# Attention and a GELU feed-forward layer on one core: scores of batch 2, two GpSimd copies and the w_out loads move

## The chip, the cores and the metric

The kernel runs on one core of one Trainium2 chip. The metric is the device time of one execution, in microseconds. The kernel before was timed five times. One execution of it was recorded by the hardware profiler, and all durations below come from that record.

## The reference

For each of 8 batches and 8 heads, a sequence x (512 x 64) and a state (32 x 64) attend to each other. Both results are concatenated along the sequence, the heads are joined into 512 columns, and a two-layer network with exact GELU follows. Cut to what matters:

```python
scores = scale * x @ state.T          # 512 x 32 per batch and head
a      = softmax(scores)
xread  = a @ state                    # 512 rows
scores2 = scale * state @ x.T
sread  = softmax(scores2) @ x         # 32 rows
y = concat([xread, sread], rows), heads joined   # 4352 x 512
h = y @ w_in                          # 512 -> 2048
out = gelu(h) @ w_out                 # 2048 -> 512, float32
```

## The kernel before

**The work of one batch.** The scores of a batch are exponentiated once into e (`scores`, L315: 16 small matmuls into two PSUM tiles pt, and two exps on ScalarE). `norm` (L337) divides by the row sums on VectorE, in two halves, and gives a. The reads of the sequence rows are not formed: state and w_in are multiplied first into P (`pmat`, L428, four pieces of 512 columns, copied out of PSUM by ScalarE and VectorE), and the hidden layer is then AT times P, where AT is a transposed. For batches from 2 on, AT is made by a DMA transpose on SP's queue (`atr_dma`, L363), and the transposed x that the scores need by another (`xtr_dma`, L268).

`mm1(b, m)` (L464) makes one of 16 row blocks of the hidden layer: two matmuls into a PSUM tile hp, and a gelu on ScalarE into row m of gs[b]. `M(k)` is mm1 with k = 16 b + m, so M(22) is row 6 of batch 1. The second layer is done in units: `U(u)` is mm2(u // 16, u % 16 // 4, u % 4), and mm2(b, q, j) (L490) multiplies the four rows m = 4 q to 4 q + 3 of gs[b] with the same rows of w_out, for one block j of 128 tokens, into one PSUM tile. U(20) is therefore mm2(1, 1, 0): rows 4 to 7 of batch 1. `mm2_m(b, m)` (L518) does one row m for all four blocks j instead. The units serve batches 0 and 1; from batch 2 on the second layer is formed with seven half-size products (`X`, L602), whose sums of w_out (`w_sums`, L545) are made once on VectorE.

`sread` (L371) multiplies e with a copy of x that has a column of ones beside it (xo). That copy is made by `rearr_ones` (L223), on GpSimd from batch 2 on, and the copy x4 that the DMA transpose reads by `rearr` (L214), on GpSimd too. Both kinds of buffer have two copies, taken in turn by the batch number.

**What sets the order.** The schedule is written out by hand (`tc.manual_schedule()`): each engine executes its instructions in the order of the calls, and semaphores are set where one engine reads what another wrote. The calls from L805 to L939 are the first two batches, the loop from L942 does the rest. PSUM tiles with the tag "f" (hp, pt, p_ps and others) come from four slots taken in turn: a new one waits until the fourth before it has been read.

**Loads.** All weights and the x of batches 1 to 7 are loaded by DMAs that GpSimd issues, in the order of the calls. `load_rest` (L133) issues the second to fourth chunks of w_in and w_out, the rest of the state, and x of batches 2 and 3. On GpSimd's queue follow rearr(2), rearr_ones(2), a one-element copy called hold (L912, which waits for row 4 of gs[1]), load_x(4), rearr(3), rearr_ones(3), the hold of L975 (which waits for row 0 of gs[2]), load_x(5) and rearr(4).

Of the kernel before, what the change touches and what calls it, by code (L numbers as in the profile page):

```python
# [17 lines left out]
def kernel(  # L18
# [8 lines left out]
    nc = tc.nc  # L27
# [27 lines left out]
    def otile(shape, name, at=None):  # L55
        if at is None:
            at = turn[0] % 4
            turn[0] += 1
        return ps_o.tile(shape, FP32, name=name, tag=f"o{at}")
# [19 lines left out]
    hold = persist.tile([128, 1], BF16, name="hold")  # L79
# [23 lines left out]
    def load_w_in(f0, f1):  # L103
        for t in range(2):
            nc.gpsimd.dma_start(
                out=w_in_bf[64 * t:64 * t + 64, :, f0:f1],
                in_=moe_w_in[256 * t:256 * t + 256, f0:f1].rearrange("(c d) f -> d c f", c=HC),
            )
# [3 lines left out]
    def load_w_out(m0, m1):  # L112
        nc.gpsimd.dma_start(out=w_out_bf[:, m0:m1, :], in_=w_out_r[:, m0:m1, :])

    def load_x(b):
        xb = xin.tile([128, H, SJ * D], BF16, name="xb", tag="xb")
        nc.gpsimd.dma_start(out=xb, in_=xr[b])
        xbs[b] = xb

    def load_st(b0, b1):  # L120
        nc.gpsimd.dma_start(
            out=st_bf[:, b0:b1, :, :].rearrange("q b t d -> q (b t) d"),
            in_=st_rows[:, b0:b1, :, :].rearrange("q b t d -> q (b t) d"),
        )
# [6 lines left out]


    def load_rest():  # L133
        load_w_out(4, 8)
        for f in range(2, FC):
            load_w_in(512 * f, 512 * f + 512)
            load_w_out(4 * f, 4 * f + 4)
        load_st(2, B)
        load_x(2)
        load_x(3)  # L140
# [82 lines left out]
    def rearr_ones(b):  # L223
        A = atts[b]
        eng = nc.vector if b < 2 else nc.gpsimd
        src = xbs[b].rearrange("p (t c) (j d) -> p t c j d", t=2, d=D)
        for t in range(2):
            eng.tensor_copy(  # L228
                out=A.xo[:, :, :, 2 + 64 * t:66 + 64 * t].rearrange("p j c d -> p c j d"),
                in_=src[:, t],  # L230
            )
# [36 lines left out]
    def xtr_dma(b):  # L268
        A = atts[b]
        nc.sync.dma_start_transpose(  # L270
            out=A.xT.rearrange("p j c n -> p (j c) n"),
            in_=A.x4.rearrange("p j c n -> p (j c n)"),
        )
# [41 lines left out]
    def scores(b, half):  # L315
        A = atts[b]
        if half == 0:
            begin_e(b)
        pt = ps_f.tile([128, SJ, 2, 2, NS], FP32, name="pt", tag="f")
        for ci in range(2):  # L320
            c = 2 * half + ci
            for j in range(SJ):
                nc.tensor.matmul(  # L323
                    pt[:, j, :, ci, :],
                    lhsT=A.xT[:, j, c, :],
                    rhs=sbd[:, b, c, :],
                    start=True,
                    stop=True,
                )
        nc.scalar.activation(  # L330
            out=A.e[:, :, 64 * half:64 * half + 64],
            in_=pt.rearrange("p j t c n -> p (j t) (c n)"),
            func=AF.Exp,
            scale=scale,
        )

    def norm(b, half):  # L337
        A = atts[b]
        G = SJ * 2
        hs = slice(64 * half, 64 * half + 64)  # L340
        e4 = A.e[:, :, hs].rearrange("p g (c n) -> p g c n", n=NS)
        cs = att.tile([128, G, 2], FP32, name="cs", tag="cs")
        nc.vector.reduce_sum(out=cs, in_=e4, axis=AX.X)  # L343
        ics = att.tile([128, G, 2], FP32, name="ics", tag="ics")
        nc.vector.reciprocal(out=ics, in_=cs)
        nc.vector.tensor_tensor(  # L346
            out=A.a[:, :, hs].rearrange("p g (c n) -> p g c n", n=NS),
            in0=e4,
            in1=ics[:, :, :].to_broadcast((128, G, 2, NS)),
            op=ALU.mult,  # L350
        )
# [11 lines left out]
    def atr_dma(b):  # L363
        A = atts[b]
        A.AT = att.tile([128, SJ, 2, 128], BF16, name="AT", tag="AT")
        nc.sync.dma_start_transpose(
            out=A.AT.rearrange("p j t n -> p (j t) n"), in_=A.a
        )
# [29 lines left out]
    def srt(b):  # L398
        A = atts[b]
        ps = ps_f.tile([128, HC, NS], BF16, name="srT", tag="f")  # L400
        nc.tensor.transpose(
            ps.rearrange("p c n -> p (c n)"), A.srm.rearrange("q t d -> q (t d)"), ident
        )
        nc.vector.tensor_copy(out=XSR[:, :, :, b], in_=ps)
# [23 lines left out]
    def pmat(b, f):  # L428
        p_copy(b, f, p_mm(b, f, ftile))
# [32 lines left out]
    gs = {}  # L462

    def mm1(b, m):  # L464
        if m == 0:
            gs[b] = gpool.tile([128, MC, S], BF16, name="g", tag="g")
        hp = ps_f.tile([128, S], FP32, name="hp", tag="f")
        for t in range(2):
            nc.tensor.matmul(  # L469
                hp,  # L470
                lhsT=Ps[b][:, t, m * 128:(m + 1) * 128],
                rhs=atts[b].AT[:, :, t, :],
                start=(t == 0),
                stop=(t == 1),
            )
        nc.scalar.activation(out=gs[b][:, m, :], in_=hp, func=AF.Gelu)  # L476
# [13 lines left out]
    def mm2(b, q, j):  # L490
        if q == 0:
            ops[b, j] = otile([128, d_model], "op")
        ps = ops[b, j]
        for m in range(4 * q, 4 * q + 4):
            nc.tensor.matmul(  # L495
                ps,
                lhsT=gs[b][:, m, j * 128:(j + 1) * 128],
                rhs=w_out_bf[:, m, :],
                start=(m == 0),
                stop=(m == MC - 1),  # L500
            )
        if q == 3:
            rows = out_rows(b, j)
            evac(ps, [(rows, slice(0, 128), 0, d_model)])
# [13 lines left out]
    def mm2_m(b, m):  # L518
        for j in range(SJ):
            if m == 0:  # L520
                ops[b, j] = otile([128, d_model], "op")
            nc.tensor.matmul(  # L522
                ops[b, j],
                lhsT=gs[b][:, m, j * 128:(j + 1) * 128],
                rhs=w_out_bf[:, m, :],
                start=(m == 0),
                stop=(m == MC - 1),
            )
# [16 lines left out]
    def w_sums(i):  # L545
        (b11, b12), (b21, b22) = w_q
        w_add(*(
            ("3", b12, b22, ALU.subtract),
            ("4", b21, b11, ALU.subtract),
            ("6", b11, b12, ALU.add),  # L550
            ("1", b11, b22, ALU.add),
            ("7", b21, b22, ALU.add),
        )[i])
# [243 lines left out]
    def M(*ms):  # L797
        for m in ms:
            mm1(m // MC, m % MC)

    def U(*us):
        for u in us:
            mm2(u // 16, u % 16 // 4, u % 4)
# [24 lines left out]
    norm0(1)  # L828
    load_x(1)
    load_rest()  # L830
    nc.scalar.activation(out=gate, in_=gate, func=AF.Gelu)
    keep_warm(8)
# [38 lines left out]
    scores(1, 0)  # L871
    scores(1, 1)
    srt(0)
    U(4, 5)
    rearr_ones(1)
    U(6)
    pmat(0, 2)
    norm(1, 0)
    norm(1, 1)
    U(7)  # L880
    M(8, 9)
    sread(1)
    sread_out(1)
# [32 lines left out]
    begin(3)  # L916
    rearr(3)
    xtr_dma(3)
    rearr_ones(3)
    M(22, 23)  # L920
    scores(2, 0)
    scores(2, 1)
    U(18)
    norm(2, 0)
    norm(2, 1)
    M(24, 25)
    U(19)
    M(26, 27)
    U(20, 21)
    w_sums(1)  # L930
    M(28, 29)
    w_sums(2)
    U(22)
    atr_dma(2)
    M(30, 31)
    U(23)
    pmat(2, 3)
    w_sums(3)
# [118 lines left out]
```

## Time and profile before

| What | Value |
|---|---|
| median of five executions | 206.92 us |
| lowest and highest of the five | 206.73 and 207.49 us |
| profiled execution, whole | 207.19 us |
| its span, first to last instruction | 205.4 us |
| granted TensorE clock | 0.998 |
| TensorE, ScalarE, VectorE, GpSimd busy | 199.7, 133.0, 133.4, 61.7 us |
| one gelu of 128 x 512 on ScalarE (L476) | 601 ns, 124 of them |
| one activation table load on ScalarE | 1283 ns |
| one xo copy of GpSimd (L228), median | 1.04 us |
| AT by DMA, issue to landing, median | 3.7 us |

A line of a timeline gives the start, the length, the engine, the line of the kernel, the operation, what is written and read with shapes, how many instructions are merged, and in brackets the idle time before with the one who ended it. PE is TensorE, PEld its weight loads, ACT ScalarE, DVE VectorE, POOL GpSimd, SP the engine that issues the output and transposing DMAs. Matmuls overlap, so four of 0.38 us do not take 1.5 us: the distance from start to start counts.

### The profile page before, as it was taken

To read this page: it belongs to the slowest core of one execution; us is meant where nothing else is said; L and a number is where in the kernel's file an instruction comes from. 1 tells how busy PE (TensorE), PEld (TensorE's weight loads), DVE (VectorE), ACT (ScalarE), POOL (GpSimd) and SP (SyncE) were. 2 spreads that over 40 slices of the span, in tenths; PEclk is the share of its full clock that TensorE was granted. 3 is DMA by queue.
4 is the path that set the end of the run, shared out by engine and by line. 5 is a ranking of instruction groups with operands and counts; after the bars stand their busy time and mean duration, and the time that the engine had idled before them with its cause. 6 is when DMAs were issued, how large, how long until landed. Compare 5 with 4: busy or idle time off the path is not lost.

```text
span 205.4 us, 4667 instructions
## 1 busy us (share of the span) xinstructions
PE 199.7 (97%) x1952; PEld 132.2 (64%) x1959; DVE 133.4 (65%) x218; ACT 133.0 (65%) x241; POOL 61.7 (30%) x68
## 2 busy tenths in 40 slices
PE   7899999999999999999999999999999999999994
PEld 6554544444344567766775777667775788778893
DVE  2752575885776767976697757765778553165883
ACT  4574676679795879665967687587857476744120
POOL 8694300746060305271626602330220001200000
PEclk9999999999999999999999999999999999999999
DMA  5999999679655917742594405350109001030125
GB/s 191 204 195 180 199 195 193 113 232 164 97 63 144 228 28 99 161 152 56 67 151 142 106 0 116 112 134 3 51 10 199 3 0 51 3 153 0 54 99 158
DMA packets 39733, 23.14 MB, mean 113 GB/s; under 512 B 21792, under 2 KB 37792, under 8 KB 39712
## 3 DMA queue, kind: packets, MB, share of 16 engines
q0 software_dynamic: 13408, 8.10, 28.5%
q1 hardware_dynamic: 25616, 14.16, 28.5%
q10 hardware_dynamic: 688, 0.59, 0.8%
q8 instruction: 15, 0.25, 0.5%
q14 instruction: 6, 0.05, 0.1%
HBM read 17.30 MB, written 8.91 MB: 128 GB/s over the span
## 4 chain that ended last, share of the span: by engine, by line
PE 93%; DMA 4%; DVE 1%; SPq 0%; issue 0%
PE xp L577 34%; PE hp L469 26%; PE op L495 9%; PE p_ps L414 5%; PE op L522 3%; PE hps L509 3%; PE rp L753 3%; DMA x0f<-in_x_dram 3%; DMA AT<-a 2%; PE xp L683 2%; PE pt L323 2%; PE sr L377 1%; PE hp L848 1%; PE warm_ps L146 1%; PE aT_ps L360 1%; PE xT_ps L263 0%
## 5 line engine op out<-in xcount | busy, mean ns | idle before, releaser
L476 ACT ACTIVATE g<-hp 128x512 bf16<-128x512 f32 x124 | 66.9, 601 | 27.8 <-PE hp L469 22.2
L469 PE MATMUL hp<-AT,P 128*128 128x512 bf16 x248 | 63.6, 379 | 0.4 <-DMA AT<-a 0.3
L577 PEld LDWEIGHTS <-gsum 128*128 128x128 bf16 x448 | 43.4, 98 | 11.1 <-issue 1.9
L571 DVE TENSOR_TENSOR gsum<-g 128x2048 bf16<-128x2048 bf16 x30 | 38.6, 1305 | 0.1
L469 PEld LDWEIGHTS <-P 128*128 128x128 bf16 x248 | 22.8, 98 | 21.2 <-issue 2.5
L577 PE MATMUL xp<-ws,gsum 128*128 128x256 bf16 x256 | 30.6, 273 | 0.0
L426 DVE CAST P<-p_ps 128x512 bf16<-128x512 f32 x31 | 20.1, 685 | 10.5 <-PE p_ps L414 10.4
L495 PE MATMUL op<-w_out_bf,g 128*128 128x512 bf16 x91 | 22.9, 379 | 0.2
L577 PE MATMUL xp<-ws,g 128*128 128x256 bf16 x192 | 22.9, 273 | 0.0
L577 PE MATMUL xp<-w_out_bf,gsum 128*128 128x256 bf16 x192 | 22.8, 273 | 0.0
L425 ACT CAST P<-p_ps 128x512 bf16<-128x512 f32 x31 | 16.9, 596 | 7.6 <-PE p_ps L414 7.4
L577 PEld LDWEIGHTS <-g 128*128 128x128 bf16 x192 | 18.8, 98 | 4.3
L626 POOL TENSOR_TENSOR u<-s,oh 128x512 f32<-128x512 f32 x5 | 6.6, 1311 | 41.0 <-ACT oh L623 41.0
L228 POOL COPY xo<-xb 128x1024 bf16<-128x1024 bf16 x12 | 14.5, 1236 | 12.8 <-PE sr L377 12.8
L495 PEld LDWEIGHTS <-g 128*128 128x128 bf16 x96 | 9.0, 98 | 11.2 <-issue 1.1
L218 POOL COPY x<-xb 128x1024 bf16<-128x1024 bf16 x12 | 12.1, 1043 | 10.6 <-DMA xb<-in_x_dram 10.6
L596 POOL TENSOR_TENSOR v<-q,oh 128x512 f32<-128x512 f32 x5 | 7.1, 1428 | 20.8 <-ACT oh L628 20.8
L343 DVE TENSOR_REDUCE cs<-e 128x16 f32<-128x512 bf16 x14 | 9.5, 677 | 3.8 <-ACT e L330 3.8
L414 PE MATMUL p_ps<-w_in_bf,sbd 64*32 64x512 bf16 x256 | 10.9, 389 | 0.0
L620 DVE TENSOR_TENSOR s<-xp,s 128x512 f32<-128x512 f32 x5 | 3.5, 692 | 11.3 <-PE xp L577 11.3
L346 DVE TENSOR_TENSOR a<-e,ics 128x512 bf16<-128x512 bf16 x14 | 10.2, 730 | 0.5
L599 DVE TENSOR_TENSOR oh<-xp,v 128x512 f32<-128x512 f32 x5 | 3.5, 692 | 9.2 <-POOL v L596 9.2
(108 smaller groups left out, 220.2 us busy)
## 6 DMA issues: line engine op xcount, KB each, us to landing
xb<-in_x_dram POOLq DMA_DIRECT2D x7, 512.0 KB, 6.0
out_dram<-oh SPq DMA_DIRECT2D x13, 256.0 KB, 2.4
out_dram<-osb SPq DMA_DIRECT2D x10, 256.0 KB, 3.4
out_dram<-oh SPq DMA_DIRECT2D x5, 512.0 KB, 2.8
w_in_bf<-in_moe_w_in_dram POOLq DMA_DIRECT2D x8, 256.0 KB, 9.2
w_out_bf<-in_moe_w_out_dram POOLq DMA_DIRECT2D x3, 512.0 KB, 13.2
x0f<-in_x_dram ACTq DMA_DIRECT2D x2, 256.0 KB, 3.9
x0f<-in_x_dram SPq DMA_DIRECT2D x2, 256.0 KB, 4.6
```

Source lines behind the costliest of these rows:

```text
L218: nc.gpsimd.tensor_copy(out=A.x4[:, :, :, 64 * t:64 * t + 64].rearrange("p j c d -> p c j d"), in_=src[:, t],)
L228: eng.tensor_copy(out=A.xo[:, :, :, 2 + 64 * t:66 + 64 * t].rearrange("p j c d -> p c j d"), in_=src[:, t],)
L343: nc.vector.reduce_sum(out=cs, in_=e4, axis=AX.X)
L346: nc.vector.tensor_tensor(out=A.a[:, :, hs].rearrange("p g (c n) -> p g c n", n=NS), in0=e4, in1=ics[:, :, :].to_broadcast((128, G, 2, NS) ...
L414: nc.tensor.matmul(ps[t][32 * c:32 * c + 32, :], lhsT=sbd[64 * t:64 * t + 64, b, c, 32 * t:32 * t + 32], rhs=w_in_bf[64 * t:64 * t + 64, c ...
L425: nc.scalar.copy(out=dst[:, 0, :], in_=ps[0])
L426: nc.vector.tensor_copy(out=dst[:, 1, :], in_=ps[1])
L469: nc.tensor.matmul(hp, lhsT=Ps[b][:, t, m * 128:(m + 1) * 128], rhs=atts[b].AT[:, :, t, :], start=(t == 0), stop=(t == 1),)
L476: nc.scalar.activation(out=gs[b][:, m, :], in_=hp, func=AF.Gelu)
L495: nc.tensor.matmul(ps, lhsT=gs[b][:, m, j * 128:(j + 1) * 128], rhs=w_out_bf[:, m, :], start=(m == 0), stop=(m == MC - 1),)
L571: nc.vector.tensor_tensor(out=t, in0=g_q(b, h0, k0), in1=g_q(b, h1, k1), op=op)
L577: nc.tensor.matmul(ps[:, j - js[0], :], lhsT=lhs[:, m, 128 * j:128 * j + 128], rhs=rhs[:, m, :], start=(first and j == js[0] and m == 0), ...
```

## The change

Four things are edited. The w_out chunks of `load_rest` are loaded as two halves each. The second chunk of w_out is used row by row for batch 0: mm2_m(0, 4) to mm2_m(0, 7) stand where U(4) to U(7) stood. The two scores of batch 2 stand ahead of M(22,23) and not behind; the units U(19), U(20) and U(21) each stand one place further up between the pairs of M that follow. And rearr_ones(3) moves from behind xtr_dma(3) to behind M(30,31), with a new hold ahead of it that waits for row 15 of gs[1].

```diff
     def load_rest():
-        load_w_out(4, 8)
+        load_w_out(4, 6)
+        load_w_out(6, 8)
         for f in range(2, FC):
             load_w_in(512 * f, 512 * f + 512)
-            load_w_out(4 * f, 4 * f + 4)
+            load_w_out(4 * f, 4 * f + 2)
+            load_w_out(4 * f + 2, 4 * f + 4)
...
     srt(0)
-    U(4, 5)
+    mm2_m(0, 4)
+    mm2_m(0, 5)
     rearr_ones(1)
-    U(6)
+    mm2_m(0, 6)
     pmat(0, 2)
     norm(1, 0)
     norm(1, 1)
-    U(7)
+    mm2_m(0, 7)
...
     xtr_dma(3)
-    rearr_ones(3)
-    M(22, 23)
     scores(2, 0)
     scores(2, 1)
     U(18)
     norm(2, 0)
     norm(2, 1)
+    M(22, 23)
+    U(19)
     M(24, 25)
-    U(19)
+    U(20)
     M(26, 27)
-    U(20, 21)
+    U(21)
     w_sums(1)
     M(28, 29)
     w_sums(2)
     U(22)
     atr_dma(2)
     M(30, 31)
+    nc.gpsimd.tensor_copy(out=hold, in_=gs[1][:, 15, 0:1])
+    rearr_ones(3)
     U(23)
```

## The prediction

> **What bounds the kernel now.** I read the page's busy times first, then the waits of TensorE, then the timelines of the stretch that the change rewrites.
>
> ```profile
> PE 199.7 (97%) x1952; PEld 132.2 (64%) x1959; DVE 133.4 (65%) x218; ACT 133.0 (65%) x241; POOL 61.7 (30%) x68
> ```
>
> TensorE is busy 199.7 of 205.4 us. The same 1,952 matmuls stay, so a change of order can only remove or add time in which TensorE waits. The waits of TensorE (engine, line, releaser: total, times, longest) are these:
>
> ```profile
> PE warm_ps L146 <- DVE warm L92: 1.0, 1, 1.0
> PE xT_ps L250 <- DVE x0b L236: 0.4, 1, 0.4
> PE pc L284 <- DVE xT L253: 0.3, 1, 0.3
> PE hp L469 <- DMA AT<-a: 0.3, 1, 0.3
> ```
>
> Three lie in the first 9 us, which no edit touches. The fourth is the only one within reach: M(32) waits for the DMA that transposes batch 2's attention weights (atr_dma(2)). TensorE's timeline there (start, length, line, tiles, count):
>
> ```profile
> 44.62 0.41 PE L414 MATMUL p_ps<-w_in_bf,sbd 64*32 64x512 bf16 x8
> 44.97 1.04 PE L469 MATMUL hp<-AT,P 128*128 128x512 bf16 x4
> 45.84 0.63 PE L323 MATMUL pt<-sbd,xT 128*128 128x64 bf16 x16
> 46.30 1.03 PE L495 MATMUL op<-w_out_bf,g 128*128 128x512 bf16 x4
> 47.17 1.03 PE L469 MATMUL hp<-AT,P 128*128 128x512 bf16 x4
> 48.03 0.81 PE L495 MATMUL op<-w_out_bf,g 128*128 128x512 bf16 x3
> 48.90 1.03 PE L469 MATMUL hp<-AT,P 128*128 128x512 bf16 x4
> 49.76 1.89 PE L495 MATMUL op<-w_out_bf,g 128*128 128x512 bf16 x8
> ...
> 55.03 0.41 PE L414 MATMUL p_ps<-w_in_bf,sbd 64*32 64x512 bf16 x8
> 55.74 1.04 PE L469 MATMUL hp<-AT,P 128*128 128x512 bf16 x4 [0.30 <-DMA AT<-a]
> ```
>
> Read the starts, not the lengths: four matmuls take 0.863 us from start to start (48.90 to 49.76), 0.216 each; sixteen score matmuls take 0.46. After p_ps the next matmul starts 0.35 later (44.62 to 44.97), so M(32) was due at 55.03 + 0.35 = 55.38 and started at 55.74: the wait is worth 0.36. ScalarE in the same stretch:
>
> ```profile
> 45.10 0.59 ACT L425 CAST P<-p_ps 128x512 bf16<-128x512 f32 x1 [0.58 <-PE p_ps L414]
> 45.61 1.08 ACT L476 ACTIVATE g<-hp 128x512 bf16<-128x512 f32 x2
> 46.71 1.28 ACT L330 ACT_TABLE_LOAD   x1
> 48.00 1.09 ACT L330 ACTIVATE e<-pt 128x512 bf16<-128x512 f32 x2
> 49.11 1.28 ACT L476 ACT_TABLE_LOAD   x1
> 50.40 2.06 ACT L476 ACTIVATE g<-hp 128x512 bf16<-128x512 f32 x4
> ```
>
> Around two exps ScalarE makes no gelu from 46.69 to 50.40: two table loads and two exps. Gelus of M(22) and M(23) (line 2) come before that hole. Two rows of SP's queue show the transposes:
>
> ```profile
> 47.78 3.03 SPq L270 DMA_TRANSPOSE xT<-x  x1
> 52.01 2.30 SPq L366 DMA_TRANSPOSE AT<-a  x1
> ```
>
> **What the Trainium skill says.** "ScalarE: Activation LUTs", What ACT_TABLE_LOAD costs, gives 1283 ns for a load and another 1380 ns of drain. The trace agrees on the load (1.28), but the exp starts 0.01 us after it (46.71 + 1.28, then 48.00): I take 1.28 without the drain. "Perfetto Trace Analysis", Sequencer Loop, has an engine instruction wait for its semaphore after it was queued; the trace agrees that what stands behind it waits too, since after the held M(32) no matmul starts before 55.74. "SBUF — State Buffer", SBUF: two separate sides, calls the port pair of VectorE and GpSimd an exclusive lock; the trace fits that: GpSimd's xo copies last 1.04 us at their median, and one that starts beside a gsum of VectorE (90.13) lasts 1.92.
>
> **The scores of batch 2 sooner.** They move ahead of M(22,23): four matmuls of hp, 0.86 us. They then start at 44.97. On ScalarE the cast ends at 45.69 and the exp load follows at once: 45.70 to 46.98. The two exps run 46.99 to 48.08, the gelu load 48.10 to 49.38, gelu M(22) 49.39 to 49.99 (0.60 for a single one), gelu M(23) 0.49 later, to 50.48. So the exps come 1.01 us sooner, but gelus 22 and 23 end at 49.99 and 50.48 where they ended at 46.20 and 46.69.
>
> The norms follow the exps. Norm 2 ends on VectorE at 51.94 now (the transpose is issued at 52.01) and at about 50.93 then. SP is free from 47.78 + 3.03 = 50.81, so atr_dma(2) is issued at about 51.0 and lands, 3.7 us later (the median of AT<-a), at 54.7. M(32) is not due before 55.38: the wait of 0.36 goes. If the transpose of batch 3's x holds it up, 0.7 us is spare, and more with what follows.
>
> **The units moved up.** The diff does a second thing: U(20) now stands before M(26,27), with only M(22,23), U(19) and M(24,25) between the scores and it. U(20) is mm2(1, 1, 0), which multiplies rows m = 4 to 7 of gs[1]. M(16) starts batch 1, so rows 6 and 7 are what gelus M(22) and M(23) write. In the kernel before they had ended three microseconds ahead of U(20) (46.69 against 49.76). In the order as built, U(20)'s third and fourth weight loads now each wait for ScalarE. TensorE's schedule: scores 44.97, U(18) 45.43, M(22,23) 46.29, U(19) 47.16, M(24,25) 48.02, U(20) 48.88. Its third matmul is due at 49.31 and its fourth at 49.53. The fourth's weights are released at about 50.48 + 0.04 = 50.52, and the matmul starts up to 0.11 later (a load of 0.10 with its gap): at 50.52 to 50.63. It is late by 1.0 to 1.1 us. I take 1.08, as the L469 loads released by a ScalarE cast (26.16, loaded from 26.20, matmul at 26.31) show the longer form. Behind it TensorE's whole queue waits: M(26,27), U(21) and all that follows. Nothing later gives it back: by the list above TensorE waits for no engine and no DMA after 55.74, so the delay reaches the end.
>
> The PSUM slots add nothing. M(24,25) reuse the slots of the scores, freed by the exps at 47.59 and 48.08, before 48.02 and 48.45. M(26,27) reuse those of M(22,23), freed by the same gelus that held U(20). Later gelus follow at 0.49 each and are ahead.
>
> **Batch 3's x with ones, and the new hold.** Two GpSimd copies (2.02 us) leave 47.69 and stand behind a copy that waits for gelu M(31), which ends at 54.93 now and about 55.65 then. With the hold (0.2 to 0.8) they end near 58, or near 60 at 1.92 each beside w_sums. The queue behind them is hold L975 (now 57.17), load_x(5) (57.69) and rearr(4) (58.56 to 60.58); these slip by 1 to 3 us. The next reader, xtr_dma(4), is issued at 65.34 behind output DMAs on SP: spare 2 us at worst. load_x(5) is not wanted before rearr(5) near 78, xo(3) not before sread(3) near 90. Cost 0; if VectorE is blocked instead, w_sums slip by up to 1 us and their first reader is at 70.
>
> **Rows of the second chunk and halves.** U(4) to U(7) and the four mm2_m calls hold the same sixteen matmuls: 0. TensorE waits for no weights in this trace, so there is nothing to save in it. The halves add three DMA issues on GpSimd at about 0.73 us (1.45 for the two halves already there): 2.2 us, before a queue that idles anyway:
>
> ```profile
> 21.50 0.87 POOL L117 DMA_DIRECT2D xb<-in_x_dram  x1 [2.17 <-DMA w_out_bf<-in_moe_w_out_dram]
> 35.94 2.02 POOL L218 COPY x<-xb 128x1024 bf16<-128x1024 bf16 x2 [10.59 <-DMA xb<-in_x_dram]
> ```
>
> The first row also shows that each of these DMAs waits for the one eight before it. With three more, the last w_in piece waits for load_x(1) (landed by 18.30) and load_x(2) for a w_in piece (landed at 24.3 by the trace's semaphore records). The engines move 190 to 200 GB/s through 10 to 30 us, and some 2 MB stay queued, so landings stay: 0. The tightest is the last w_in piece: landed 29.8, read at 30.36. If cover fails there, up to 0.6 us.
>
> **Sum.** +1.08 - 0.36 = +0.72 us. The profiled execution took 207.19 us, span 205.4 with 1.8 around it: it would become 207.9. It stands 0.27 above the median of the five; on the median, 206.92 + 0.72 gives 207.6. Its own range is 207.4 to 207.9: a stall of 0.95 to 1.15, and an AT wait of 0.2 to 0.5.
>
> **Rivals.** *The transposed weights are usually later than traced.* The five times spread over 0.76 us, and if that is the AT wait, the median execution could lose 0.7 to 1.1 there. The new wait of 1.08 takes its place: near 206.9, the same. Against it: the profiled execution is the second slowest and waits 0.36.
>
> *The second w_out chunk comes late in executions without a profile, and the halves cure it: faster.* It landed just before 21.50 and U(4) reads it at 22.41, 0.9 us of cover. Row by row, rows 6 and 7 are wanted eight matmuls (1.73 us) later. To come out below the bound (about 0.2%, 0.41 us, is what a measurement of this kernel can tell from no change) it must save 0.72 + 0.41 = 1.13, so the chunk must land after 23.5, two microseconds later than traced. It would give about 206.4. For it: transfers fill the DMA engines here. Against it: w_in pieces have less cover (0.6 and 0.8) and would hold TensorE first.
>
> *The halves throttle the loads.* The last w_in piece lands after 30.36 by 0.6 or so: about 208.3.
>
> **Chances.** Forecast 0.70 (0.67 of it above the bound), same 0.15, faster 0.07, throttled 0.08. The range 206.9 to 208.0 leaves out the faster case, most of the throttled one and little else. Faster 0.07, same 0.18, slower 0.75.
>
> **What would show it.** In the profile after: no TensorE wait on AT<-a; a new wait of TensorE's loads on ACT g near 49.3, about 1 us, in front of the L497 matmuls; gelus resuming at 49.4. Wrong if U(20) runs four matmuls 0.216 apart, if M(32) still waits, or if L416 waits for w_in.

## The result, and the profile after

| | before | after |
|---|---|---|
| median | 206.78 us (80 executions) | 207.49 us (43 executions) |
| lowest and highest | 205.9 and 208.85 us | 206.2 and 208.71 us |
| ratio after to before | | 1.0029, 95% interval 1.0017 to 1.0042 |
| span of the profiled execution | 205.4 us | 205.0 us |

The change makes the kernel slower by 0.29%, which is 0.60 us on 206.78 (0.35 to 0.87 by the interval). The two medians lie 0.71 us apart, which is inside the interval; the ratio is that of the fast executions. The forecast was +0.72 us.

One number seems to contradict this: the profiled execution of after has the shorter span. Read the span in three parts. From the first instruction to M(20)'s first matmul it took 42.80 us before and 41.76 after. From there to M(32)'s first matmul, the stretch that the change rewrites, it took 12.94 and 13.57. From M(32) to the end it took 149.68 and 149.66. The first part varied over the twelve profiles of this study, from 41.76 to 43.19 in those with w_out in halves and from 42.51 to 43.09 in those with whole chunks. These ranges overlap, so one profile says nothing about it. The last part lay between 149.66 and 149.71 in all twelve. So the kernels differ in the middle: 13.57 - 12.94 = +0.63 us, close to the 0.60 of the ratio. For the comparisons below I use that middle part and call it the stretch. Times "after M(20)" count from M(20)'s first matmul.

The busy times of after, against those of before:

```profile
PE 198.1 (97%) x1952; PEld 130.9 (64%) x1959; DVE 136.0 (66%) x218; ACT 133.1 (65%) x241; POOL 65.8 (32%) x72
```

The same 1,952 matmuls, and four more instructions on GpSimd: three DMA issues and one hold. The waits of TensorE in after (engine, line, releaser: total, times, longest):

```profile
PE xT_ps L252 <- DVE x0b L238: 1.3, 3, 0.6
PE warm_ps L148 <- DVE warm L92: 1.0, 1, 1.0
PE op L497 <- ACT g L478: 0.6, 1, 0.6
PE pc L286 <- DVE xT L255: 0.3, 1, 0.3
```

The wait on AT is gone from the list. In its place a unit matmul (op, L497) waits for a gelu. Its size does not stand in this line, because part of the lost time lies under the modelled length of the matmul before it. TensorE's timeline from M(24,25) on gives it (start, length, line, tiles, count, and idle time with its releaser):

```profile
46.99 1.03 PE L471 MATMUL hp<-AT,P 128*128 128x512 bf16 x4
48.07 0.38 PE L497 MATMUL op<-w_out_bf,g 128*128 128x512 bf16 x1
49.00 0.88 PE L497 MATMUL op<-w_out_bf,g 128*128 128x512 bf16 x2 [0.55 <-ACT g L478]
49.72 1.03 PE L471 MATMUL hp<-AT,P 128*128 128x512 bf16 x4
...
54.99 0.41 PE L416 MATMUL p_ps<-w_in_bf,sbd 64*32 64x512 bf16 x8
55.33 1.04 PE L471 MATMUL hp<-AT,P 128*128 128x512 bf16 x4
```

From M(24,25) at 46.99, two groups of four at 0.863 each put M(26,27) at 48.72. It starts at 49.72, so the stall is 1.00 us. It cuts U(20) in two: two of its matmuls (one record is missing) run by 48.3, two from 49.00. M(32) starts 0.34 after p_ps, as it does where it waits for nothing. The weight loads of U(20) and ScalarE's work show why:

```profile
49.00 0.10 PEld L497 LDWEIGHTS <-g 128*128 128x128 bf16 x1 [1.04 <-ACT g L478]
49.49 0.10 PEld L497 LDWEIGHTS <-g 128*128 128x128 bf16 x1 [0.39 <-ACT g L478]
```

```profile
44.06 0.59 ACT L427 CAST P<-p_ps 128x512 bf16<-128x512 f32 x1 [0.58 <-PE p_ps L416]
44.66 1.28 ACT L332 ACT_TABLE_LOAD   x1
45.95 1.08 ACT L332 ACTIVATE e<-pt 128x512 bf16<-128x512 f32 x2
47.06 1.28 ACT L478 ACT_TABLE_LOAD   x1
48.35 3.08 ACT L478 ACTIVATE g<-hp 128x512 bf16<-128x512 f32 x6
```

Gelus M(22) and M(23) are the first two of the last line. They end at 48.95 and 49.44, and each of the two loads starts 0.05 later. The chain of waits, cut to this stretch (start, length, what), says the same from the other end. Here it leaves TensorE and runs through ScalarE for 4.8 us, with pauses of at most 0.02:

```profile
44.66 1.28 ACT L332
...
45.95 1.08 ACT e L332 x2
...
47.06 1.28 ACT L478
...
48.35 1.09 ACT g L478 x2
...
49.49 0.39 PE op L497
```

SP's two transposes, of batch 3's x and of batch 2's weights:

```profile
46.74 3.36 SPq L272 DMA_TRANSPOSE xT<-x  x1
50.21 1.25 SPq L368 DMA_TRANSPOSE AT<-a  x1
```

AT's issue starts 8.44 us after M(20), where it was 9.20 before (52.01 - 42.80). But by the trace's semaphore records it lands at 54.79, which is 13.03 after M(20), against 12.89 before. This is the part that the forecast did not have.

### The profile page after: what moved, and what is told of

Its sections match the earlier page's. It is cut to its first block, busy times and chain, and to the rows that moved or that the text cites. A ratio compares the mean times of both kernels' runs of the same rounds, so it can differ in the third digit from the quotient of the medians.

```text
span 205.0 us, 4673 instructions
## 1 busy us (share of the span) xinstructions
PE 198.1 (97%) x1952; PEld 130.9 (64%) x1959; DVE 136.0 (66%) x218; ACT 133.1 (65%) x241; POOL 65.8 (32%) x72
## 4 chain that ended last, share of the span: by engine, by line
PE 91%; ACT 4%; DMA 2%; DVE 1%; issue 1%; SPq 0%
PE xp L579 34%; PE hp L471 26%; PE op L497 7%; PE op L524 5%; PE p_ps L416 5%; PE hps L511 3%; PE rp L755 3%; DMA x0f<-in_x_dram 2%; PE xp L685 2%; PE pt L325 1%; PE sr L379 1%; PE hp L850 1%; ACT L478 1%; ACT L332 1%; ACT L833 1%
## 5 line engine op out<-in xcount | busy, mean ns | idle before, releaser
L579 PEld LDWEIGHTS <-g 128*128 128x128 bf16 x192 | 18.8, 98 | 4.3
L497 PE MATMUL op<-w_out_bf,g 128*128 128x512 bf16 x76 | 19.5, 380 | 0.8 <-ACT g L478 0.6
L230 POOL COPY xo<-xb 128x1024 bf16<-128x1024 bf16 x12 | 15.5, 1323 | 10.8 <-PE sr L379 10.8
L497 PEld LDWEIGHTS <-g 128*128 128x128 bf16 x80 | 7.6, 98 | 10.8 <-ACT g L478 1.4
L348 DVE TENSOR_TENSOR a<-e,ics 128x512 bf16<-128x512 bf16 x14 | 12.0, 860 | 0.5
L524 PE MATMUL op<-w_out_bf,g 128*128 128x512 bf16 x45 | 11.4, 380 | 0.2
```

Source lines behind the costliest of these rows:

```text
L230: eng.tensor_copy(out=A.xo[:, :, :, 2 + 64 * t:66 + 64 * t].rearrange("p j c d -> p c j d"), in_=src[:, t],)
L348: nc.vector.tensor_tensor(out=A.a[:, :, hs].rearrange("p g (c n) -> p g c n", n=NS), in0=e4, in1=ics[:, :, :].to_broadcast((128, G, 2, NS) ...
L497: nc.tensor.matmul(ps, lhsT=gs[b][:, m, j * 128:(j + 1) * 128], rhs=w_out_bf[:, m, :], start=(m == 0), stop=(m == MC - 1),)
L524: nc.tensor.matmul(ops[b, j], lhsT=gs[b][:, m, j * 128:(j + 1) * 128], rhs=w_out_bf[:, m, :], start=(m == 0), stop=(m == MC - 1),)
L579: nc.tensor.matmul(ps[:, j - js[0], :], lhsT=lhs[:, m, 128 * j:128 * j + 128], rhs=rhs[:, m, :], start=(first and j == js[0] and m == 0), ...
```

## The experiments

The theory: the whole effect lies in the new order of the stretch. The gelus of M(22) and M(23) now stand behind two table loads, and U(20) reads their rows. The rivals: the rest of the edits (halves, rows, GpSimd copies) costs or saves time, or it is only that U(20) reads these rows, so that U(20)'s old place would cure it.

**e1_stretch_only: the kernel before, with nothing but the new order.**

```diff
-    M(22, 23)
     scores(2, 0)
     scores(2, 1)
     U(18)
     norm(2, 0)
     norm(2, 1)
-    M(24, 25)
+    M(22, 23)
     U(19)
+    M(24, 25)
+    U(20)
     M(26, 27)
-    U(20, 21)
+    U(21)
```

> The kernel before with the new order of scores(2), M and U alone; loads, rows of the second chunk and rearr_ones(3) as before. Theory (U(20) waits for gelus M(22), M(23) that now lie behind two table loads; AT wait goes): the whole effect is here, +0.6 to +0.7 us, ratio 1.003, and from the first matmul of pmat(2,2) to M(32) 11.75 us, against 11.12 in the kernel before. Rival (the copy of batch 3's x beside w_sums, or the split loads, cost it): ratio 1.000 here. Second rival (rearr_ones(3) in its old place holds up the transpose of the attention weights): a wait for AT as well, over 1.005.

Measured: ratio 1.0027 (1.0009 to 1.0045). The stretch took 13.57, as in after. TensorE's timeline around the stall:

```profile
48.60 0.59 PE L495 MATMUL op<-w_out_bf,g 128*128 128x512 bf16 x2
49.75 0.88 PE L495 MATMUL op<-w_out_bf,g 128*128 128x512 bf16 x2 [0.55 <-ACT g L476]
```

Here all four records of U(20) are present: two matmuls, a gap, two more. The new order alone gives the effect of the whole change.

**e2_rest_only: the changed kernel, with the old order of that stretch.** The same lines turned back:

```diff
     xtr_dma(3)
+    M(22, 23)
     scores(2, 0)
...
-    M(22, 23)
-    U(19)
     M(24, 25)
-    U(20)
+    U(19)
     M(26, 27)
-    U(21)
+    U(20, 21)
```

> The changed kernel with the old order of scores(2), M and U; split loads, row by row and the late rearr_ones(3) stay. Theory: no effect, ratio 0.999 to 1.001, a wait on AT of about 0.36 us again and 11.1 us from pmat(2,2) to M(32). Rival (these parts cost): ratio 1.003. Rival (row by row hides late weights in executions without a profile): below 0.998.

Measured: ratio 1.0012 (0.9987 to 1.0038), a stretch of 13.06. Of the waits of TensorE, the stall on the gelu is gone and the one on AT is back:

```profile
PE hp L471 <- DMA AT<-a: 0.4, 1, 0.4
```

The stretch is 0.12 longer than in the kernel before, as AT landed 0.12 later after M(20) (13.01, not 12.89). The halves, the rows and the moved GpSimd copies have no effect that can be measured; the interval leaves room for 0.13% less and 0.38% more.

**e3_unit_back: the changed kernel, with U(20) behind M(26,27) again.**

```diff
     M(24, 25)
-    U(20)
     M(26, 27)
-    U(21)
+    U(20, 21)
```

> The changed kernel with U(20) behind M(26,27) again, so no unit reads gelus M(22), M(23) early. Theory, as refined: only four PSUM slots exist, M(26) needs the slot of M(22) and waits for the same gelu, so the stall only changes its place and label (hp waits on ACT g) and stays at about 1.0 us; ratio 1.003. Rival (the data that U(20) reads are the whole cause): the stall goes, AT does not wait, ratio 0.998.

Measured: ratio 1.0046 (1.0026 to 1.0067), a stretch of 13.77. TensorE's timeline:

```profile
47.12 1.03 PE L471 MATMUL hp<-AT,P 128*128 128x512 bf16 x4
49.13 1.08 PE L471 MATMUL hp<-AT,P 128*128 128x512 bf16 x4 [0.98 <-ACT g L478]
50.05 1.89 PE L497 MATMUL op<-w_out_bf,g 128*128 128x512 bf16 x8
```

With U(20) out of the way, M(26) waits, and for the same gelu: it takes the PSUM slot that M(22) filled, the fourth before it. It was due at 47.12 + 0.86 = 47.98 and starts at 49.13, so the stall is 1.15. The data of U(20) is the first thing that the late gelus hold and not the only one. The rival falls: what costs is that ScalarE makes no gelu during 3.7 us of loads and exps, whichever reader of the late gelus comes first. Whether more than four slots would shorten the stall was not tried.

**e6_no_table: the changed kernel, with no table loads around batch 2's scores.** The two activations of these scores compute a gelu, so that batch 2's exponential is left out.

```diff
-            func=AF.Exp,
+            func=AF.Gelu if b == 2 else AF.Exp,
```

> The changed kernel with Gelu in place of Exp in the two activations of batch 2's scores, so that ScalarE needs neither table load there; it leaves out the exponential of batch 2. Theory (the two loads of 1.28 us make the hole): gelu M(22) ends 2.6 us sooner, U(20) runs without a stall, no AT wait: from M(20) to M(32) 12.55 us, against 13.57 in the changed kernel and 12.94 before; ratio 0.998. Rival (the two exps or the order of ScalarE's queue alone are the cause): a stall of half a microsecond or more is left.

Measured: ratio 0.9986 (0.9962 to 1.0009), a stretch of 12.92. ScalarE's timeline, and then TensorE's:

```profile
45.56 1.09 ACT L332 ACTIVATE e<-pt 128x512 bf16<-128x512 f32 x2
46.92 1.08 ACT L478 ACTIVATE g<-hp 128x512 bf16<-128x512 f32 x2 [0.26 <-PE hp L471]
```

```profile
55.01 0.41 PE L416 MATMUL p_ps<-w_in_bf,sbd 64*32 64x512 bf16 x8
55.70 1.04 PE L471 MATMUL hp<-AT,P 128*128 128x512 bf16 x4 [0.28 <-DMA AT<-a]
```

Half of the expectation held. Without the table loads the gelus follow the exps as soon as TensorE has filled their tile (0.26), and the stall is gone: the two loads make it. The other half failed. AT still made M(32) wait, although the exps ended sooner than in after. In the profile the kernel came out no better than before. The next two runs move a transpose.

**e7_xt_sooner: the changed kernel, with batch 3's x transposed ahead of M(20,21).** A rival for AT's late landing was that its transfer shares the DMA engines with that of batch 3's x, which now overlaps it more.

```diff
     U(16)
+    begin(3)
+    rearr(3)
+    xtr_dma(3)
     M(20, 21)
...
-    begin(3)
-    rearr(3)
-    xtr_dma(3)
     scores(2, 0)
```

> The changed kernel with rearr(3) and the transpose of batch 3's x moved from behind pmat(2,2) to ahead of M(20,21), so that this transpose is done before the one of the attention weights is issued. Theory (in the changed kernel the attention weights land late, 13.0 us after M(20), because the two transposes share the DMA engines; the wait is only covered by the stall): they land 11.5 to 12.2 us after M(20); the stall of 1.0 and the time from M(20) to M(32) stay at 13.57, ratio 1.003. Rival (their transpose takes 4.6 us anyway): landing stays at 12.9 to 13.0.

Measured: ratio 1.0032 (1.0014 to 1.0051), a stretch of 13.57. The transpose of x had landed at 50.56, before AT was issued (51.38). AT still took 4.57 us from issue to landing, as in after (4.58), and landed 12.76 after M(20), not 11.5 to 12.2. Sharing with that transpose is not what makes the way longer.

**e8_no_table_xt: both edits, e6 and e7, together.**

> The changed kernel with Gelu in place of Exp for batch 2 (it leaves out the exponential of batch 2), as in the run without table loads, and in addition the transpose of batch 3's x ahead of M(20,21). Theory: neither stall nor AT wait is left, 12.55 us from M(20) to M(32), ratio 0.998. Rival: an AT wait of 0.3 us as in the run without table loads, 12.9.

Measured: ratio 0.9988 (0.9965 to 1.001), a stretch of 12.57. AT was issued 6.78 after M(20) and landed at 11.53, 4.75 after its issue. On TensorE's timeline p_ps starts at 54.72 and M(32) at 55.06, 0.34 later. With neither stall nor AT wait, 12.57 is what TensorE's own work in the stretch takes. The kernel before spends 0.37 more than that, its AT wait. The changed kernel spends 1.00 more, its stall. The two do not add: the stall comes first on TensorE's queue, and M(32) is late enough through it that AT has landed.

**e4_unit_kept: the changed kernel, with U(17), a unit that is ready, kept to fill the hole.**

```diff
     M(20, 21)
-    U(17)
...
     M(24, 25)
+    U(17)
     U(20)
```

> The changed kernel with U(17) taken from ahead of the scores and put between M(24,25) and U(20): 0.86 us of matmuls that need no new gelu, in the stall. Theory: of the 1.0 us stall 0.9 is filled, 0.1 to 0.3 left (the second half of the scores may wait 0.2 for its slot), no AT wait: 0.1 to 0.3 us faster than the kernel before, ratio 0.999, and 0.8 us faster than the changed one. Rival (the cost is not this stall): ratio stays at 1.003.

Measured: ratio 1.0003 (0.9978 to 1.0027), a stretch of 12.89. The stall shrank to 0.10: the eight matmuls of U(17) and U(20) ran from 48.12 to 49.94, 1.82 instead of 1.73. It was filled, 0.09 over. But without U(17) ahead of them the scores came 0.86 sooner in TensorE's order, and their second half waited for its PSUM slot: 44.66 - 43.97 = 0.69 from the scores to the next group, instead of 0.46. The two, 0.09 and 0.23, make up the 12.89 - 12.57 = 0.32 over TensorE's own work (e8). Of the expected gain of 0.1 to 0.3 on the kernel before, 0.05 is left in the profile, and none in the ratio.

**e5_before_kept: the kernel before, with U(17) behind the scores.** It lets the scores start sooner and leaves gelus 22 and 23 ahead of the table loads.

```diff
     M(20, 21)
-    U(17)
...
     norm(2, 1)
+    U(17)
     M(24, 25)
```

> The kernel before with one edit: U(17) moves from ahead of pmat(2,2) to behind the scores of batch 2, so everything from pmat(2,2) to the exps comes up to 0.86 us sooner, and gelus M(22), M(23) stay ahead of the table loads. Theory: no stall on a gelu, and the transposed weights land about 0.6 us sooner, so the AT wait of 0.36 goes: from M(20) to M(32) 12.6 to 12.7 us against 12.94, ratio 0.998 to 0.9985. Rival (any sooner score brings a stall, or the landing of AT is set by the transpose of batch 3's x and not by its issue): 12.9 or more, ratio 1.000 or more.

Measured: ratio 1.0005 (0.9984 to 1.0027), a stretch of 12.89. The expected gain did not come. TensorE's timeline:

```profile
44.11 1.06 PE L469 MATMUL hp<-AT,P 128*128 128x512 bf16 x4
45.06 0.88 PE L323 MATMUL pt<-sbd,xT 128*128 128x64 bf16 x16
45.77 1.89 PE L495 MATMUL op<-w_out_bf,g 128*128 128x512 bf16 x8
...
55.36 0.41 PE L414 MATMUL p_ps<-w_in_bf,sbd 64*32 64x512 bf16 x8
55.70 1.04 PE L469 MATMUL hp<-AT,P 128*128 128x512 bf16 x4
```

The AT wait is gone (0.34 from p_ps to M(32)). But M(22,23) took 44.11 to 45.06, 0.09 over its 0.86, and the scores 45.06 to 45.77, 0.25 over their 0.46, because their PSUM slots were not yet read (by the gelu of M(21) and the two copies of P, by the releasers that the trace names). One wait of 0.37 was exchanged for two that add up to 0.34.

**e9_kept_split and e10_kept_split_xt: a unit between the two scores.** e9 is e5 with U(18) between scores(2, 0) and scores(2, 1), so that the second slot has time to be read. e10 is e9 with the transpose of batch 3's x moved as in e7.

```diff
     scores(2, 0)
-    scores(2, 1)
     U(18)
+    scores(2, 1)
     norm(2, 0)
```

> The kernel before with U(17) behind the scores of batch 2, as in the run that kept U(17) back, and U(18) between the two halves of the scores, so that the second half does not wait for its PSUM slot. Theory: the slot wait of 0.25 goes; the attention weights land 12.7 us after M(20) as in that run, so a wait for them of 0.1 to 0.2 may appear: 12.65 to 12.8 us from M(20) to M(32), ratio 0.999. Rival: time unchanged at 12.9, because the AT wait takes the place of the slot wait fully.

> As the run before it, and the transpose of batch 3's x ahead of M(20,21). Theory: the attention weights land within 12 us of M(20), no wait for them; 12.6 to 12.65 us from M(20) to M(32), 0.3 us less than in the kernel before, ratio 0.9985, the best of all. Rival: the earlier copy and transpose of batch 3's x collide with those of batch 2 and a wait for xT appears at the scores: 12.9 or more.

Measured: e9 0.9993 (0.9976 to 1.0011) with a stretch of 12.71; e10 0.998 (0.9964 to 0.9995) with a stretch of 12.64. TensorE's timeline of e10:

```profile
44.82 0.39 PE L323 MATMUL pt<-sbd,xT 128*128 128x64 bf16 x8
45.05 1.03 PE L495 MATMUL op<-w_out_bf,g 128*128 128x512 bf16 x4
...
54.88 0.41 PE L414 MATMUL p_ps<-w_in_bf,sbd 64*32 64x512 bf16 x8
55.22 1.04 PE L469 MATMUL hp<-AT,P 128*128 128x512 bf16 x4
```

The first half of the scores takes its 0.23 (44.82 to 45.05; the second too, 45.92 to 46.15), and M(32) follows p_ps by 0.34. Both stretches came out as expected. e10 took 206.22 us against 206.79 for the kernel before beside it, with an interval that ends just below 1: by the ratio and by the 0.30 us of the profile it is faster than the kernel before, by little, and so faster than the change. It keeps what the change gave up: gelus 22 and 23 run before the tables are switched, and it moves work that waits for nobody behind the scores.

## Why the prediction was right, and the step that failed

The forecast, slower by 0.72 us from a new stall of TensorE on ScalarE, was right: the chip gave 0.60 (0.35 to 0.87), the stretch of the profile 0.63. Step by step, on the time after M(20):

- **The exps come sooner, the gelus later: right.** Forecast for the exps 46.99 - 42.80 = 4.19, measured 45.95 - 41.76 = 4.19. Forecast for the end of gelu M(23) 50.48 - 42.80 = 7.68, measured 49.44 - 41.76 = 7.68. Such a chain of one engine without waits can be added up to a hundredth from its own rows. The table load without the drain was right: the exps follow it by 0.01. e6 shows by removal that the two loads make the hole.
- **U(20) waits for rows 6 and 7: right, 0.08 too long.** The stall was 1.00 where I took 1.08 from the range 1.0 to 1.1. The load took 0.05 from the end of the gelu, and the matmul came with it, not 0.11 behind.
- **The wait on AT goes: it did, but for another reason than the one given.** This is the step that failed, in the words "atr_dma(2) is issued at about 51.0 and lands, 3.7 us later (the median of AT<-a), at 54.7: the wait of 0.36 goes". Forecast for the landing 54.7 - 42.80 = 11.9 after M(20); measured 13.03, no sooner than before. Of the 1.13 that are missing, 0.24 is a later issue (8.44 instead of 8.20: SP was busy 3.36 with the transpose of x, not 3.03), and 0.88 is a longer way from issue to landing (4.58, not 3.7; what stood in the way is below). Without the stall M(32) would have been due at 55.33 - 1.00 = 54.33, 0.46 ahead of AT's landing at 54.79. So the wait went because the stall covered it, and the sooner scores gained nothing; in e6, where nothing stalls, the wait is there (0.28). The reserve of 0.7 us that the prediction named for a late AT was too small; "what follows", the stall, gave the rest. That this term came out right is luck as far as its reason goes. The sum came out right since only the later of the two delays counts: 1.00 - 0.37 = 0.63.
- **The PSUM slots add nothing: right as long as U(20) stands first.** The same gelus hold M(26), as e3 shows, and there they cost 1.15.
- **GpSimd's copies and the hold: cost 0, right, with more slip than I had named.** Below, GpSimd's queue in after, and VectorE's beside it. Before, the two xo copies took 2.02, the hold 0.24 and the product of batch 3's norm 0.69.

```profile
55.14 3.09 POOL L230 COPY xo<-xb 128x1024 bf16<-128x1024 bf16 x2
58.17 1.18 POOL L980 COPY hold<-g 128x1 bf16<-128x1 bf16 x1
59.29 0.87 POOL L117 DMA_DIRECT2D xb<-in_x_dram  x1
60.16 2.02 POOL L220 COPY x<-xb 128x1024 bf16<-128x1024 bf16 x2
```

```profile
56.11 3.19 DVE L545 TENSOR_TENSOR ws<-w_out_bf 128x2048 bf16<-128x2048 bf16 x2
59.22 0.67 DVE L345 TENSOR_REDUCE cs<-e 128x16 f32<-128x512 bf16 x1
...
60.22 2.51 DVE L348 TENSOR_TENSOR a<-e,ics 128x512 bf16<-128x512 bf16 x1
```

Counted from M(20), the copies end at 58.23 - 41.76 = 16.47, between the two forecasts (58 and 60, that is 15.2 and 17.2), and load_x(5) slips by (59.29 - 41.76) - (57.69 - 42.80) = 2.64 us. I had not named that rearr(4) then meets the norm's product, which takes 2.51 and ends 2.6 us later than before. Nobody waits for it: the last part of the span is as long as before.
- **Rows and halves: 0, right.** TensorE waits for no weights in after, and e2 finds no effect. (The page gives 180 to 199 GB/s from 10 to 30 us, not 190 to 200; nothing rests on it.)
- **The rivals.** That AT is usually later than traced, and that the halves cure a late chunk, both need a gain in unprofiled executions that hides the stall. The ratio of e1, 1.0027 with none of the halves, and that of e2, 1.0012 with all of them, leave room for a gain of some 0.1% at most (e2's interval begins at 0.9987). There is a hint that such waits exist: the profile of e5, which has whole w_out chunks and started early (its first hidden-layer matmul at 11.82), shows TensorE waiting for the third chunk of w_out and for the last piece of w_in:

```profile
28.02 1.89 PE L522 MATMUL op<-w_out_bf,g 128*128 128x512 bf16 x7 [0.26 <-DMA w_out_bf<-in_moe_w_out_dram]
```

```profile
30.37 0.14 PEld L414 LDWEIGHTS <-sbd 64*32 64x32 bf16 x15 [0.44 <-DMA w_in_bf<-in_moe_w_in_dram]
```

The profile of after started as early (11.81), has halves, and shows neither wait. But it is not the second chunk, on which that rival rested, and one profile of each does not show that the halves are the reason. *The halves throttle the loads* was wrong: the last piece of w_in holds nothing in after.

**Why AT did not land sooner, and what stays open.** In the seven kernels with the scores ahead of M(22,23) (after, e1, e3, e4, e6, e7, e8), SP's issue took 1.23 to 1.25 us, and AT landed 3.9 to 4.8 after it began. In the five others the issue took 2.2 to 2.5 and the landing 3.5 to 3.8. Sharing with the transpose of x is excluded by e7 and e8, and the table loads by e6 and e8. The DMA records of the traces show something else. In all twelve, one packet of 16 KB, of a kind that the profile calls "instruction", moves while AT is on its way. In after it takes from 52.08 to 53.32. Two lines of the DMA view of after, from 50 to 55 us in 40 slices, show the rate of all DMAs and that packet:

```profile
GB/s 164 281 287 293 293 289 295 287 289 287 293 128 197 229 209 217 336 213 217 188 166 102 18 0 0 0 4 8 10 8 10 10 37 4 0 0 0 0 0 0
q8 instruction: 1, 0.02, 1.6%
```

By 52.9 all but 44 of AT's 1,024 packets of 256 bytes have moved. These 44 move only after the instruction packet has ended, at some 10 GB/s, and AT lands at 54.79. In ten of the twelve kernels about half of AT's packets were left when the instruction packet ended, and AT landed 1.80 to 1.87 after that end; in after and e7, with 44 and 28 left, 1.41 to 1.46 after it. The issue took 2.2 to 2.5 where the packet began 0.52 to 0.69 after the issue did, and 1.23 to 1.25 where it began 0.75 or more after it. The six transposes of attention weights in each trace make 72. The 36 with no instruction packet ahead of their last data landed 3.43 to 3.72 after their issue began, the 36 with one 3.52 to 5.41. So the median of 3.7 is the way of an undisturbed transpose. No run moves that packet on purpose: its part is read from the traces and not shown by an experiment. What sets its moment (8.7 us after M(20) in e8, 9.2 in e10, 9.7 to 10.3 in the others) stays open.

## What to carry to other kernels

A switch of ScalarE's function is a hole for everything that ScalarE feeds, here 3.7 us without a gelu: before work is moved across it, list which results come to lie behind the hole, and who reads them or needs their buffers within its length. Give to the hole what needs neither (U(17) in e10), and keep what the next readers want ahead of it. And a wait that goes from the list may only be covered by a new one: compare when its releaser lands, not whether the line is there. Before a DMA's median time is added to a sooner issue, see whether that median holds where the DMA will run: here 3.7 became 4.58.

## What the runs showed of the hardware that was not expected

In e1 a product of VectorE with two inputs in SBUF took 1.63 us instead of 0.69 beside two GpSimd copies that ran from 47.40 to 49.42. VectorE's line:

```profile
48.34 1.63 DVE L346 TENSOR_TENSOR a<-e,ics 128x512 bf16<-128x512 bf16 x1
```

The second copy ends at 49.42, and the product 0.55 after it, at 49.97. "SBUF — State Buffer", SBUF: two separate sides, says that one of the two takes the shared port pair for its whole instruction while the other is fully blocked; the lengths agree, since the product ends most of its own 0.69 after the copy. That the one that starts first takes it, as that section also says, does not fit: the product began at 48.34 and the second copy at 48.38, and the product still ended last. Nobody waited for it: e1's stretch is as long as that of after. In after the other side lost too: two copies took 3.09 instead of 2.02, and a copy of a single column 1.18 instead of 0.24, beside the sums of w_out.
